# Other SBUF addresses for the same program: feed-forward buffers at multiples of 2048 bytes, attention buffers at multiples of 128

## The chip, the cores and the metric

The kernel runs on one core of a Trainium2 chip. A core has a matrix engine (TensorE, in the profile PE, with its weight loads listed apart as PEld), a vector engine (VectorE, DVE), a scalar engine (ScalarE, ACT), GpSimd (POOL), and a sync engine (SP) that here issues all the DMA transfers. The engines work on the on-chip memory SBUF, 128 partitions that are addressed alike: the address of a buffer is a byte offset that is the same in every partition. TensorE writes its results to a second memory, PSUM, in eight banks. The metric is the device time of one launch in microseconds (us); lower is better.

## What is computed

A linear attention over 8 batches, 8 heads, 576 positions and 64 channels, whose result feeds a gated feed-forward layer on 4608 tokens (512 to 1536 to 512). Everything is float32.

```python
def phi(x):
    proj = np.einsum('bhsd,df->bhsf', x, w_phi)
    proj = proj - np.max(np.abs(proj), axis=-1, keepdims=True)
    return np.concatenate([np.exp(proj), np.exp(-proj)], axis=-1)
q_p, k_p = (phi(q), phi(k))
kv = np.einsum('bhsf,bhsd->bhfd', k_p, v)
z = np.sum(k_p, axis=2)
num = np.einsum('bhsf,bhfd->bhsd', q_p, kv)
den = np.einsum('bhsf,bhf->bhs', q_p, z)[..., None] + 1e-06
attn = num / den
# x: attn as 4608 tokens of 512 channels
gate = 1.0 / (1.0 + np.exp(-(x @ w_gate)))
val = x @ w_val
out = gate * val @ w_out
```

## The kernel before

The work is cut in two kinds. Attention: 32 steps, one for a batch and a pair of heads (`attention(i)`). Its matmuls are float32: `pk` and `pq` (projections of k and q), `kvz` (kv and z), `tp` (transposes), `nm` and `dp` (numerator and denominator), `px` (spreading of maxima). Feed-forward: 9 chunks of 512 tokens by 12 blocks of 128 hidden channels (`unit(S_, C, j)`). Every operand is split into a high and a low part of type float32r, x into `xh` and `xl`, the weights into `wh` and `wl`, the hidden values into `hh` and `hl`, and three products stand for one: high by high, high by low, low by high. A matmul of the feed-forward has a stationary operand of 128 columns (512 bytes of a partition), which is loaded first, and a moving operand of 512 columns (2048 bytes). A unit has 12 matmuls for the gate (`g`), 12 for the value (`v`), which hold the weights still and move x (line 755), and then 12 for the output (`acc`, line 762), which hold `hh` or `hl` still and move the weights. That makes 9 x 12 x 36 = 3888 float32r matmuls of one size.

Blocks 0 to 3 are stage A: their weights `wh0` to `wl3` are made ready early, and their units fill TensorE between the steps of the attention. Blocks 4 to 11 are stage B (2592 of the 3888 matmuls); it comes when the attention is over. In the trace `gA`, `vA`, `hhA` belong to stage A and `gB`, `vB`, `hhB` to stage B. After a matmul of the gate come, on ACT and DVE, a tanh, an exp and some products (lines 797 to 824).

The order of all instructions is set when the program is built: the class `Plan` places each operation on its engine by ranks, given costs and due times, and emits them in that order. Costs and ranks don't depend on addresses.

SBUF is divided from two sides. From the left come `const` (with `ebias`), `moe` (x, t, u, hh, hl, y) and `wp1` (`wh0` to `wl3`), later replaced by four buffers `y2`. From the right come the buffers of the attention (`at1`, `at`). When the attention is done, `swap_right` gives these up and puts the weights of stage B (`wh4` to `wl11`) and their raw forms (`wraw`, `wtop`) in their place. A buffer starts at the end of its neighbour, rounded up to 32 bytes, so that one small buffer sets the remainder of all that follow. These are the addresses that come out:

| buffers | address before | remainder by 2048 / by 128 | address after | remainder by 2048 / by 128 |
|---|---|---|---|---|
| `xh`, `xl` (two of each, 8192 bytes each) | from 2208 | 160 / 32 | from 2048 | 0 / 0 |
| `t`, `u`, `hh`, `hl`, `y` of stage A (2048 each) | from 34976 | 160 / 32 | from 34816 | 0 / 0 |
| `wh0` ... `wl3` (6144 each), later `y2` | from 65696 | 160 / 32 | from 65536 | 0 / 0 |
| `wh4` ... `wl11` (6144 each) | 118752 to 217055 | 2016 / 96 | 116736 to 215039 | 0 / 0 |
| `wraw`, `wtop` of stage B | from 217056 | 2016 / 96 | from 215040 | 0 / 0 |
| `kin`, `qin`, `vin`, `wraw` and `mid` of stage A | from 121440 | several / 96 | from 118528 | several / 0 |
| `d`, `dk`, `ek`, `mb`, `kvt`, `eq`, `kv`, `ex`, `dr`, `rb`, `xp` | from 152864 | several / 32 | from 151296 | several / 0 |
| `mx`, `pm`, `pn`, `dn` (small) | from 152672 | several / 0, 32, 64 or 96 | from 149760 | several / 0 |
| `ident`, `ones`, `halves`, `wk`, `spread` | from 225888 | several / 96 | from 225536 | several / 0 |

The slices that matmuls of the feed-forward take of these buffers start at multiples of 512 bytes within them, so that a slice has the remainder of its buffer by 512, by 128 and by 64.

The functions that the diff touches:

Of the kernel before, what the change touches and what calls it, by code (L numbers as in the profile page):

```python
# [9 lines left out]
F32 = mybir.dt.float32  # L10
# [11 lines left out]
P = 128  # L22
# [8 lines left out]
HS = S // 2  # L31
Q = 32
# [122 lines left out]
def act_time(n):  # L155
    return 0.085 + n * 0.00085
# [3 lines left out]
def attention_moe(  # L160
# [10 lines left out]
    nc = tc.nc  # L171
    vec, act, pool = nc.vector, nc.scalar, nc.gpsimd
# [2 lines left out]

    const = ctx.enter_context(tc.tile_pool(name="const", bufs=1))
    dram = ctx.enter_context(tc.tile_pool(name="dram", bufs=1, space=DRAM))
    moe = ctx.enter_context(tc.tile_pool(name="moe", bufs=2))
    left, right = ExitStack(), ExitStack()
    wp1 = left.enter_context(tc.tile_pool(name="wp1", bufs=1))  # L180
    at1 = right.enter_context(tc.tile_pool(name="at1", bufs=1, side="right"))
    at = right.enter_context(tc.tile_pool(name="at", bufs=2, side="right"))
# [3 lines left out]
    homes = {"wp": wp1, "ws": at}  # L186
# [7 lines left out]
    def buf(tag, n):  # L194
        return Buf(rings.setdefault(tag, Slots(n)))
# [7 lines left out]
    ]  # L203
    dens = [dram.tile([2, S], F32, tag=f"den{i}", name=f"den{i}") for i in range(N)]

    ebias = const.tile([P, 1], F32, name="ebias")
    vec.memset(ebias, -896.0 * 2.0**23)
    ident = at1.tile([P, P], F32, name="ident")
    make_identity(nc, ident)
    ones = at1.tile([P, Q], F32, name="ones")  # L210
    vec.memset(ones, 1.0)
    halves = at1.tile([P, 2, Q], F32, name="halves")
    vec.memset(halves, 0.0)
# [2 lines left out]
    wk = at1.tile([P, F], F32, name="wk")  # L216
    nc.sync.dma_start(wk, w_phi)
    spread = at1.tile([P, 4, P], F32, name="spread")
    pool.memset(spread, 0.0)
    for a in range(4):  # L220
        qs = slice(a * Q, a * Q + Q)
# [5 lines left out]
    def head(hd):  # L227
        return slice(hd * D, hd * D + D)
# [102 lines left out]
    def attention(i):  # L331
        b, p = steps[i]
        n = f"{i}"
        T = {}
# [34 lines left out]
        mx, dk = buf("mx", 2), buf("dk", 1)  # L369
        eks = []  # L370

        def k_max():
            T["mx"] = [at.tile([P, 4], F32, tag=f"mx{g}", name=f"mx{n}_{g}") for g in range(3)]
            for g, ns in enumerate((4, 4, 1)):
                vec.tensor_reduce(
                    T["mx"][g][:, :ns], pks[g].t[:, :ns, :], axis=AX.X, op=ALU.max,
                    apply_absolute_value=True,
                )

        def k_sub():  # L380
            T["dk"], T["ek"] = [], []
            for g, ns in enumerate((4, 4, 1)):
# [6 lines left out]
                T["dk"].append(dkt)  # L389

        km = plan("DVE", 1.43, k_max, [ko], pks, [mx], rank=i)
        kb = plan("DVE", 1.43, k_sub, [km], [*pks, mx], [dk], rank=i)

# [66 lines left out]
        pm, mb = buf("pm", 2), buf("mb", 1)  # L460
        nj = 2 * S // Q

        def q_max():
            T["pm"] = at.tile([P, nj], F32, tag="pm", name="pm" + n)
            T["pn"] = at.tile([P, nj], F32, tag="pn", name="pn" + n)
            vec.tensor_reduce(
                T["pm"],
                T["d"].rearrange("p h s -> p (h s)").rearrange("p (j t) -> p j t", t=Q),
                axis=AX.X, op=ALU.max, apply_absolute_value=True, apply_transpose=True,
            )  # L470
# [30 lines left out]
        def q_sub():  # L501
            vec.tensor_tensor(T["d"], T["d"], T["mb"], op=ALU.subtract)

        q1 = plan("DVE", 1.38, q_max, qc, [d], [pm], rank=i)
        if perm:
            pp = Buf(banks, mine)
# [119 lines left out]
        if soon:  # L626

            def invert():
                dn = at.tile([P, 2 * HS // Q], F32, tag="ds", name="ds" + n)
                for hf, dp in enumerate(dps):  # L630
                    vec.tensor_reduce(
                        dn[:, hf * 9 : hf * 9 + 9], dp.t.rearrange("p (j t) -> p j t", t=Q),
                        axis=AX.X, op=ALU.max, apply_transpose=True,
                    )
                vec.tensor_scalar(dn, dn, 1e-6, None, op0=ALU.add)
                vec.reciprocal(dn, dn)
                T["rb"] = at.tile([P, S], F32, tag="rb", name="rb" + n, bufs=1)
                vec.transpose(T["rb"], dn.unsqueeze(2).broadcast_to([P, S // Q, Q]))

            r = [plan("DVE", 2.1, invert, [do], dps, [rb], rank=i - 1)]  # L640
        else:
            dr, dn = buf("dr", 1), buf("dn", 2)

            def den_copy():
                T["dr"] = at.tile([P, HS], F32, tag="dr", name="dr" + n, bufs=1)
                act.copy(T["dr"], dps[0].t)

            def den_in():
                T["dn"] = at.tile([P, 9], F32, tag="dn", name="dn" + n)
                nc.sync.dma_start(T["dn"], T["dr"].rearrange("(o r) c -> o r c", r=Q)[:, 0, :])  # L650

            def den_inv():
                vec.tensor_scalar(T["dn"], T["dn"], 1e-6, None, op0=ALU.add)
                vec.reciprocal(T["dn"], T["dn"])

            def den_out():
                nc.sync.dma_start(dens[i].rearrange("h (r c) -> (h r) c", c=9), T["dn"])

            def den_wide():
                T["rb"] = at.tile([P, S], F32, tag="rb", name="rb" + n, bufs=1)  # L660
                for hd in range(2):
                    nc.sync.dma_start(
                        T["rb"][head(hd), :], dens[i][hd].unsqueeze(0).broadcast_to([D, S])
                    )

            r = plan("ACT", act_time(HS), den_copy, [do], dps, [dr], rank=i - 0.2)
            r = plan("SP", 0.06, den_in, [r], [dr], [dn], rank=i - 2.5, mode=4)
            r = plan("DVE", 0.42, den_inv, [r], [dn], rank=i - 1)
            r = plan("SP", 0.06, den_out, [r], [dn], rank=i - 2.5, mode=4)
            r = [plan("SP", 0.12, den_wide, [r], [], [rb], rank=i - 2.5, mode=288, lag=2.5)]  # L670
# [172 lines left out]

    def swap_right():
        right.close()
        ctx.enter_context(reopen)
        for name in ("ws", "wp"):
            homes[name] = ctx.enter_context(
                tc.tile_pool(
                    name=name + "2", bufs=2 if name == "ws" else 1, side="right",  # L850
                    reuse_waits="tile",
                )
            )

    reopen = ExitStack()
    firsts = [o for n in range(3 * JA) for o in wdone[wtiles[n]]]
    swap = plan(None, 0.0, swap_right, [*every, *(s for c in stores.values() for s in c), *firsts])
    for n in range(3 * JA, 3 * NJ):
        weigh(n, 60 + n, swap)

    ydone, outs = {}, []
    for C in range(NCK):
# [5 lines left out]
        for t in range(CW // P):  # L868
            ab, yb = Buf(banks, apart), buf("y", 2)
            T = {}  # L870
# [30 lines left out]
    for C in range(NCK):  # L901
# [3 lines left out]
        for j in js:  # L905
# [3 lines left out]
            for t in range(CW // P):  # L909
# [15 lines left out]
                T = {}  # L925
# [15 lines left out]
                a = plan("DVE", vec_time(DM), add, [o, l], [accs[t], yb], rank=GATE)  # L941
                plan("SP", 0.06, store, [a], [yb], rank=90, mode=256)
    plan.run(trace)
    reopen.close()


# [53 lines left out]
```

## Time and profile before

| what | value |
|---|---|
| median of 3 runs | 1242.1 us (1240.03 to 1245.85) |
| the profiled execution | 1241.6 us, of which the span from first to last instruction is 1239.6 us |
| PE busy | 1220.3 us (98%), 8480 matmul instructions |
| DVE / ACT busy | 758.1 us (61%) / 518.1 us (42%) |
| DMA | 131.4 MB, mean 106 GB/s |
| granted TensorE clock, mean | 0.997 |

By the trace the attention, with stage A between its steps, lasts until 520 us, what is left of stage A until 616 us, and stage B from there to the end. Times in the views are microseconds from the start of the span. A matmul's duration in a row includes the time that its results need to run through the array (389 to 398 ns in the feed-forward); the next one starts long before. What a matmul costs is therefore read as the distance from one start to the next, called spacing below: where a row gathers twelve matmuls in sequence, it is a twelfth of its time.

### The profile page before, as it was taken

The numbers are of one execution on the slowest core, as the hardware profiler recorded it, in microseconds if no ns is written. First come the engines' busy times: TensorE is split into PE (matmuls) and PEld (weight loads), VectorE is DVE, ScalarE is ACT, GpSimd is POOL, SyncE is SP. The second block draws the span as 40 slices with busy tenths as digits, with TensorE's granted clock in tenths as the row PEclk, the third lists the DMA queues.
The fourth block names the chain that finished last, engine by engine and source line by source line (L and its number), as shares of the span: only waits on it lengthen the run. The fifth ranks groups of instructions, "written<-read, shape, count | busy, mean of one in ns | idle before, by whom it ended". The sixth has DMA issues, their size and how long they took to land.

```text
span 1239.6 us, 20852 instructions
## 1 busy us (share of the span) xinstructions
PE 1220.3 (98%) x8480; PEld 916.4 (74%) x8480; DVE 758.1 (61%) x1410; ACT 518.1 (42%) x1012; POOL 2.3 (0%) x11
## 2 busy tenths in 40 slices
PE   8999999999999999999999999999999999999998
PEld 6566766666666666688887888888888888888886
DVE  6989688889886889569986424333242434242333
ACT  6766566665575656544432212222222212221221
POOL 0000000000000000000000000000000000000000
PEclk9999999999999999999999999999999999999999
DMA  7776433443252533256662202011120202020100
GB/s 256 241 252 220 137 116 120 139 137 93 89 179 62 159 106 109 67 214 212 206 210 93 103 1 102 1 54 49 34 69 1 102 1 102 1 102 1 68 1 34
DMA packets 66891, 131.42 MB, mean 106 GB/s; under 512 B 16492, under 2 KB 22764, under 8 KB 64620
## 3 DMA queue, kind: packets, MB, share of 16 engines
q1 hardware_dynamic: 66796, 130.10, 32.0%
q8 instruction: 66, 1.08, 0.4%
q14 instruction: 29, 0.24, 0.1%
HBM read 92.04 MB, written 28.45 MB: 97 GB/s over the span
## 4 chain that ended last, share of the span: by engine, by line
PE 84%; DVE 10%; ACT 3%; issue 2%; DMA 1%; SPq 0%; DVEq 0%; ACTq 0%
PE acc L762 20%; PE vB L755 15%; PE gB L755 15%; PE gA L755 6%; PE vA L755 6%; PE kvz L534 5%; PE nm L592 5%; PE pq L434 3%; PE dp L616 2%; PE pk L360 2%; PE kvz L551 2%; DVE wtop L283 1%; DVE wraw L298 1%; ACT wtop L279 1%; PE tp L572 1%
## 5 line engine op out<-in xcount | busy, mean ns | idle before, releaser
L809 DVE SCALAR_TENSOR_TENSOR tB<-tB,vB 128x512 f32<-128x512 f32 x72 | 49.5, 687 | 208.0 <-PE vB L755 208.0
L820 ACT CAST hhB<-uB 128x512 fp32r<-128x512 f32 x72 | 44.7, 620 | 304.1 <-DVE uB L813 304.1
L762 PE MATMUL acc<-wh,hhB 128*128 128x512 f32 x288 | 114.5, 398 | 2.2 <-ACT hhB L820 2.2
L762 PE MATMUL acc<-wh,hlB 128*128 128x512 f32 x288 | 114.2, 397 | 0.7 <-DVE hlB L824 0.7
L762 PE MATMUL acc<-wl,hhB 128*128 128x512 f32 x288 | 114.5, 397 | 0.0
L755 PE MATMUL gB<-xlB,wh 128*128 128x512 f32 x288 | 113.8, 395 | 0.0
L755 PE MATMUL gB<-xhB,wl 128*128 128x512 f32 x288 | 113.7, 395 | 0.0
L755 PE MATMUL vB<-xhB,wl 128*128 128x512 f32 x288 | 113.6, 394 | 0.0
L755 PE MATMUL gB<-xhB,wh 128*128 128x512 f32 x288 | 113.6, 394 | 0.0
L755 PE MATMUL vB<-xhB,wh 128*128 128x512 f32 x288 | 113.5, 394 | 0.0
L755 PE MATMUL vB<-xlB,wh 128*128 128x512 f32 x288 | 113.5, 394 | 0.0
L797 ACT ACTIVATE tB<-gB 128x512 f32<-128x512 f32 x72 | 43.0, 598 | 130.5 <-PE gB L755 130.5
L805 DVE TENSOR_SCALAR tB<-tB 128x512 uint32<-128x512 uint32 x72 | 30.7, 426 | 104.6 <-ACT tB L797 104.6
L399 ACT ACTIVATE ek<-dk 128x512 f32<-128x512 f32 (+1 forms) x192 | 83.0, 519 | 9.2 <-DVE dk L384 9.2
L534 PE MATMUL kvz<-ek,vin 128*32 128x256 f32 x1280 | 75.5, 381 | 2.1 <-ACT d L446 2.1
L824 DVE TENSOR_TENSOR hlB<-uB,hhB 128x512 fp32r<-128x512 f32 x72 | 49.7, 691 | 41.2 <-ACT hhB L820 41.2
L762 PEld LDWEIGHTS acc<-wh,hhB 128*128 128x128 f32 x288 | 54.6, 190 | 15.4 <-ACT hhB L820 2.7
L762 PEld LDWEIGHTS acc<-wh,hlB 128*128 128x128 f32 x288 | 54.6, 189 | 14.7 <-DVE hlB L824 2.0
L755 PEld LDWEIGHTS gB<-xhB,wh 128*128 128x128 f32 x288 | 54.0, 188 | 13.2
L762 PEld LDWEIGHTS acc<-wl,hhB 128*128 128x128 f32 x288 | 54.5, 189 | 12.5
L755 PEld LDWEIGHTS vB<-xhB,wh 128*128 128x128 f32 x288 | 53.9, 187 | 13.3
L755 PEld LDWEIGHTS gB<-xlB,wh 128*128 128x128 f32 x288 | 54.0, 187 | 13.1
(114 smaller groups left out, 2459.2 us busy)
## 6 DMA issues: line engine op xcount, KB each, us to landing
wraw<-w_moe SPq DMA_DIRECT2D x36, 512.0 KB
kin<-k SPq DMA_DIRECT2D x32, 320.0 KB
vin<-v SPq DMA_DIRECT2D x32, 320.0 KB
qin<-q SPq DMA_DIRECT2D x32, 288.0 KB
wh<-wtop SPq DMA_DIRECT2D x36, 256.0 KB
ys<-y SPq DMA_DIRECT2D x36, 256.0 KB
xlB<-xs SPq DMA_DIRECT2D x9, 1024.0 KB
y<-ys SPq DMA_DIRECT2D x36, 256.0 KB
```

The source lines that it names most:

```text
L360: nc.tensor.matmul(pks[hd].t[:, t, :], kx[head(hd), t * P : t * P + P], wk[head(hd), :], start=True, stop=True,)
L399: act.activation(e[:, :, sg * F : sg * F + F], T["dk"][g], AF.Exp, scale=1.0 - 2.0 * sg,)
L434: nc.tensor.matmul(pqs[hd].t, wk[head(hd), :], T["qin"][head(hd), hf * HS : hf * HS + HS], start=True, stop=True,)
L534: nc.tensor.matmul(z[o : o + Q, : 2 * F], vx[:, 2 * t + hd, o % D : o % D + Q], (e0, e1)[hd][:, t, :] if t < 4 else e2[:, 0, :], start=t = ...
L592: nc.tensor.matmul(nm.t[o : o + Q, :], w[:, sg, o : o + Q], es[sg][:, o // D, cs], start=sg == 0, stop=sg == 1, tile_position=(0, o),)
L755: nc.tensor.matmul(o, a[:, ws], y[:, cs], start=i == 0, stop=i == 11)
L762: nc.tensor.matmul(acc, a[:, ts], w[:, ws], start=first and i == 0, stop=last and i == 2)
L797: act.activation(T["t"], gb.t, AF.Tanh, scale=0.5)
L805: vec.tensor_scalar(tu, tu, 0x7FFFFFFF, None, op0=ALU.bitwise_and)
L809: vec.scalar_tensor_tensor(t, t, 1.0, vb.t, op0=ALU.add, op1=ALU.mult)
L820: act.copy(T["h"][0], T["u"])
L824: vec.tensor_tensor(hl, T["u"], hh.bitcast(F32), op=ALU.subtract)
```

## The change

No operation is added or taken away but for padding: `ebias` becomes a slice of a 896-byte buffer and is allocated first; the scratch area for DMA descriptors at address 0 shrinks from 2048 to 1024 bytes; small buffers (`mx`, `pm`, `pn`, `dn`, `ds`, `ones`) become slices of 256-byte buffers and `dr` of one of 1280 bytes; two unused buffers (`edge`, 224 bytes, and `edge2`, 2016 bytes) stand at the right end. The sequence of instructions on each of the five engines is the same before and after, row for row. Five instructions, at the hand-over from the attention's buffers to those of stage B, wait on a partly different set of semaphores, since other old buffers lie under the new ones: three on DVE (on `wtop4_0`, `wraw4_0`, `wtop4_1`) and two transfers on SP (the loads of `wraw4_0` and of `xlA8`, chunk 8 of x).

```diff
+    ebias = const.tile([P, 224], F32, name="ebias")[:, :1]
+    vec.memset(ebias, -896.0 * 2.0**23)
     moe = ctx.enter_context(tc.tile_pool(name="moe", bufs=2))
...
-    ebias = const.tile([P, 1], F32, name="ebias")
-    vec.memset(ebias, -896.0 * 2.0**23)
     ident = at1.tile([P, P], F32, name="ident")
     make_identity(nc, ident)
-    ones = at1.tile([P, Q], F32, name="ones")
+    ones = at1.tile([P, 2, Q], F32, name="ones")[:, 0, :]
...
     spread = at1.tile([P, 4, P], F32, name="spread")
+    at1.tile([P, 56], F32, name="edge")
...
-            T["mx"] = [at.tile([P, 4], F32, tag=f"mx{g}", name=f"mx{n}_{g}") for g in range(3)]
+            T["mx"] = [
+                at.tile([P, 64], F32, tag=f"mx{g}", name=f"mx{n}_{g}")[:, :4] for g in range(3)
+            ]
...
-            T["pm"] = at.tile([P, nj], F32, tag="pm", name="pm" + n)
-            T["pn"] = at.tile([P, nj], F32, tag="pn", name="pn" + n)
+            T["pm"] = at.tile([P, 64], F32, tag="pm", name="pm" + n)[:, :nj]
+            T["pn"] = at.tile([P, 64], F32, tag="pn", name="pn" + n)[:, :nj]
...
-                dn = at.tile([P, 2 * HS // Q], F32, tag="ds", name="ds" + n)
+                dn = at.tile([P, 64], F32, tag="ds", name="ds" + n)[:, : 2 * HS // Q]
...
-                T["dr"] = at.tile([P, HS], F32, tag="dr", name="dr" + n, bufs=1)
+                T["dr"] = at.tile([P, 320], F32, tag="dr", name="dr" + n, bufs=1)[:, :HS]
...
-                T["dn"] = at.tile([P, 9], F32, tag="dn", name="dn" + n)
+                T["dn"] = at.tile([P, 64], F32, tag="dn", name="dn" + n)[:, :9]
...
     def swap_right():
         right.close()
-        ctx.enter_context(reopen)
+        edge = reopen.enter_context(tc.tile_pool(name="edge", bufs=1, side="right"))
+        edge.tile([P, 504], F32, name="edge2")
         for name in ("ws", "wp"):
-            homes[name] = ctx.enter_context(
+            homes[name] = reopen.enter_context(
...
-    reopen = ExitStack()
+    reopen = ctx.enter_context(ExitStack())
...
-    nc = bacc.Bacc("TRN2", target_bir_lowering=False, num_devices=1, dynamic_dma_scratch_size=2048)
+    nc = bacc.Bacc("TRN2", target_bir_lowering=False, num_devices=1, dynamic_dma_scratch_size=1024)
```

More of the change, by code (lines that the diff above doesn't have):

```diff
@@ L943, in attention_moe @@
     plan.run(trace)
-    reopen.close()
 def kernel(**inputs):
```

## The prediction

> **What bounds the kernel now.** I read the page first, then the busy times by stage, the chain of work, and the timeline at the places where stages meet.
>
> ```profile
> span 1239.6 us, 20852 instructions
> PE 1220.3 (98%) x8480; PEld 916.4 (74%) x8480; DVE 758.1 (61%) x1410; ACT 518.1 (42%) x1012; POOL 2.3 (0%) x11
> PE 84%; DVE 10%; ACT 3%; issue 2%; DMA 1%; SPq 0%; DVEq 0%; ACTq 0%
> ```
>
> TensorE is busy 98% of the span and is 84% of the chain that ends last. By stage (columns: length, then busy time and instructions of PE, PEld, DVE, ACT, POOL, then granted clock, DMA share, GB/s):
>
> ```profile
> 20.00:520.00 500.00, 492.35 (x5247) 329.32 (x5239) 414.78 (x823) 316.42 (x654) 0.00 (x0) 1.00 0.45 142
> 520.00:600.00 80.00, 79.93 (x355) 65.85 (x352) 63.50 (x118) 34.49 (x61) 0.00 (x0) 1.00 0.55 189
> 700.00:1200.00 500.00, 500.00 (x2150) 402.91 (x2149) 182.87 (x298) 116.25 (x205) 0.00 (x0) 1.00 0.14 47
> ```
>
> In the attention PE is busy 492 of 500 us and DVE 415, from then on PE without a gap at full granted clock. In stage B, DVE (183 of 500) and ACT (116) have room to spare. So the time is the number of matmuls times their spacing, and a change of addresses acts through the spacing or not at all. The spacing is not one number:
>
> ```profile
> 533.94 2.72 PE gA L755 x12
> 539.38 5.45 PE acc L762 x24
> 673.07 2.80 PE vB L755 x12
> 675.87 2.80 PE gB L755 x12
> 681.47 2.79 PE acc L762 x12
> ...
> 692.62 2.80 PE gB L755 x12
> ```
>
> These are pieces of the chain (start, length, twelve or twenty-four matmuls). At the end of stage A a matmul costs 2.72 / 12 = 226.7 ns (5.45 / 24 = 227.1 in the output), in stage B 2.80 / 12 = 233.3, with the same shape, type and clock. From the row of 700 to 1200 us: 500.00 / 2149 = 232.7 ns, the mean of stage B. What differs? First, the other engines in two such pieces:
>
> ```profile
> 533.94:536.66 2.72, 2.72 (x13) 2.25 (x13) 1.38 (x2) 0.00 (x0) 0.00 (x0) 1.00 0.99 401
> 673.07:675.87 2.80, 2.80 (x13) 2.25 (x13) 0.00 (x0) 0.00 (x0) 0.00 (x0) 1.00 0.00 0
> ```
>
> The quick piece has the DMA engines at 99% and DVE at half; in the slow one nothing runs but PE. The surroundings are not the cause. Second, the place where it turns (start, duration):
>
> ```profile
> 615.00 0.39 PE L762 MATMUL acc<-wl,hhA 128*128 128x512 f32 x1
> ...
> 615.90 0.39 PE L762 MATMUL acc<-wh,hlA 128*128 128x512 f32 x1
> 616.13 0.40 PE L755 MATMUL gB<-xhB,wh 128*128 128x512 f32 x1
> ...
> 617.30 0.39 PE L755 MATMUL gB<-xhB,wl 128*128 128x512 f32 x1
> ```
>
> Five spacings up to 616.13 make 1.13 us (226), the five after it 1.17 (234). It turns at the very first matmul whose weights lie in the buffers of stage B. What sets these apart in the table of addresses is the remainder by 128: 32 for x and the weights in stage A, 32 for x but 96 for the weights in stage B. The stationary operand of the next matmul is loaded while the present one reads its moving operand:
>
> ```profile
> 1227.85 0.39 PE L755 MATMUL vB<-xhB,wl 128*128 128x512 f32 x1
> 1227.85 0.19 PEld L755 LDWEIGHTS vB<-xhB,wh 128*128 128x128 f32 x1
> ```
>
> Both start at 1227.85. Two reads of SBUF run side by side, and how they lie to each other seems to cost 6 ns a matmul. Third, the end of the kernel, where the granted clock has fallen to half:
>
> ```profile
> 1232.49:1234.62 2.13, 2.13 (x6) 1.65 (x5) 1.30 (x2) 0.00 (x0) 0.00 (x0) 0.50 0.15 58
> 1232.49 0.63 PE L762 MATMUL acc<-wh,hhB 128*128 128x512 f32 x1
> ...
> 1234.20 0.63 PE L762 MATMUL acc<-wl,hhB 128*128 128x512 f32 x1
> ```
>
> Four spacings make 1.71 us, 427 ns each, of which half is 213.5. That is the spacing at full clock if nothing were in the way, 512 columns at 2.4 a nanosecond. So 13.2 ns in stage A and 19.2 in stage B are lost to something that vanishes when the array reads half as fast. That fits reads that get in each other's way.
>
> **The change part by part.** *The weights of stage B* come from remainder 96 to 0, x and h from 32 to 0: both operands then have equal remainders, as in stage A now. I take A's measured spacing: 232.7 - 226.7 = 6.0 ns, by 2592 matmuls, 15.6 us, all on the path, since PE has no gap there.
>
> *Stage A*: remainders equal before (32 and 32) and after (0 and 0). I take no change. Bounds: no row shows two operands at 0, so either way by one step of 6.0 over 1296 matmuls, 7.8 us, and down to 213.5 (13.2 x 1296 = 17.1).
>
> *Matmuls of the attention*, 8480 - 3888 = 4592 instructions:
>
> ```profile
> 517.46 0.67 PE L592 MATMUL nm<-d,kv 128*32 128x288 f32 x8
> 517.95 0.67 PE L592 MATMUL nm<-eq,kv 128*32 128x288 f32 x8
> 518.43 0.67 PE L592 MATMUL nm<-d,kv 128*32 128x288 f32 x8
> 518.92 0.67 PE L616 MATMUL dp<-eq,kv 128*32 128x288 f32 x8
> ```
>
> Eight take 1.46 / 3 = 0.487 us, four 243 ns. Four run at once in quarters of the array. At two passes over 288 columns 576 / 2.4 = 240 would be the least, so at most 3 ns in 243 can be won: 4592 / 4 x 3 = 3.4 us. I take 0, since slower reads seem to leave nothing to win; the opposite bound is the same 3.4.
>
> *DVE and ACT* read and write at new addresses too. In the attention DVE idles 85 of 500 us; that idle time hides a few per cent of change either way. If it were gone, each per cent of DVE's 415 us would cost 4 us. In stage B it would take DVE at more than twice its time. 0 taken.
>
> *Transfers*: all sizes and their order stay. What PE waits for a transfer is once, at the start:
>
> ```profile
> PE pk L360 <- DMA kin<-k: 4.3, 1, 4.3
> ```
>
> So between 0 and 4.3 us could be won there, and a transfer a tenth slower would cost 0.4. 0 taken. The smaller descriptor scratch holds nothing here: the page's queue table names only hardware and instruction queues.
>
> *The five changed waits* stand where the first weights of stage B are made. Behind the waiting loads on SP stand the next weight loads; who waits for those is DVE, then PE:
>
> ```profile
> L304 DVE SCALAR_TENSOR_TENSOR wl<-wraw x24: 691/693/696, 544.5 to 669.2; 128x512 fp32r<-128x512 uint32 x24
> 698.23 2.79 PE acc L762 x12
> ```
>
> The last low part of the weights is done at 669.9 and first used at 698.2 (its block comes last): 28 us of cover. Until then PE gains (698 - 616) x 6.0 / 232.7 = 2.1 us on them. Cover stays, cost 0; without it, each microsecond late is one at the end.
>
> *Padding, the earlier memset of `ebias`* (one instruction at the start, while the first load is awaited): 0.
>
> Sum, against the profiled execution's 1241.6 us (0.5 below the median of the runs): 1241.6 - 15.6 = 1226.0.
>
> **The rivals.** *The start in itself counts.* Stage A's 226.7 and B's 233.3 differ by 6.67 ns, 16 columns of four bytes, 64 bytes. If reads go in pieces of 64 bytes, a row of 2048 bytes that starts at remainder 32 or 96 touches 33 pieces, and one at 0 touches 32. Then A's spacing drops by 6.7 as well, to 220.0, and B's by 12.7: 12.7 x 2592 + 6.7 x 1296 = 41.6 us, 1200.0. For it: both spacings are multiples of 6.67 (34 and 35). Against it: no aligned matmul in the trace; the 64 bytes may as well be the length of a round of banks, in which only the two operands' difference matters.
>
> *All is lost to the start*: 213.5 everywhere, 19.2 x 2592 + 13.2 x 1296 = 66.9 us, 1174.7. Against it: one piece of 64 bytes is worth half of 13.2. The Trainium skill (TensorE: Matmul & The Clock Gate, Back-to-back issue gap) gives an isolated warm spacing of N / 2.4 + 2.5 ns, so 215.8 here; by it this rival would come to an estimated 1183.
>
> *No change*: it isn't the remainder but the region. The weights of stage A lie below 115 KB, those of B between 118 and 217 KB, before and after. Then 1241.6. For it: in the trace region and remainder change together, so nothing separates them. Against it: the piece at 675.87 reads block 10 of the first chunk (weights from 192 KB on) and the one at 692.62 block 4 of the second (from 118 KB on), and both take 2.80; a matter of region should show steps within B. The Trainium skill speaks for no change, too: SBUF — State Buffer (Specifications) has lines of 16 bytes, of which 32 and 96 are multiples, and the Trainium skill's TensorE: Matmul & The Clock Gate (Step-by-step: what each phase is for) says that loading the next weights doesn't take read bandwidth from the running matmul. The trace's 2.72 against 2.80 with nothing else running is not explained by either.
>
> *Slower*: if both reads starting on a boundary always hit the same bank first, equal remainders at 0 would cost a further step of 6.0 instead of saving one, in A as in B: 6.0 x 3888 = 23.3 us, 1264.9. It decides once B's spacing passes 232.7 + 6.2 / 2592 us = 235.1. Against it: A has equal remainders now and is the quicker stage.
>
> **How the numbers follow.** Equal remainders as in A (1226.0): 0.42, the only one with a measured spacing. The start itself (1200.0): 0.20. The full floor (1174.7): 0.08. No change (1241.6): 0.15. Slower (1264.9): 0.08. The remaining 0.07 are mixtures, 0.05 of them gains and 0.02 within the bound. A measurement of this kernel can tell about 0.5%, 6.2 us, from no change. Faster 0.42 + 0.20 + 0.08 + 0.05 = 0.75, no change 0.17, slower 0.08. The range leaves out the floor and the slower case (0.16) and goes from the start's 1200.0 less the 3.4 of the attention's matmuls, 1196, to the no-change case with the median's 0.5 and the same 3.4 as a loss, rounded down to 1244. The likeliest case's own range is 1218 to 1234 (A's step of 7.8 either way).
>
> **What would show it.** In the changed profile's chain, twelve matmuls of `gB` and `vB` at 2.72 us, and 500 us of stage B holding some 2205 of them instead of 2149: right. 2.64 in both stages: the start itself counts. 2.80 in B: region. Above 2.82: the slower case. The attention should still end near 520 us and stage B begin near 616; if these move, stage A's spacing or DVE has changed. I am wrong if the difference between the operands isn't what the step at 616.13 came from, or if an absolute start matters, which nothing before can show.

## The result, and the profile after

The changed kernel takes 1229.8 us (median of 4 runs, 1227.1 to 1232.4), the kernel before beside it 1242.2 (4 runs, 1240.0 to 1245.9). The ratio is 0.9897, 95% interval 0.9865 to 0.9929: 12.4 us less. The profiled execution took 1229.7 us. From its page, the span, the busy times and the chain's shares:

```profile
span 1227.8 us, 20852 instructions
PE 1204.3 (98%) x8480; PEld 916.1 (75%) x8480; DVE 757.1 (62%) x1410; ACT 517.2 (42%) x1012; POOL 2.3 (0%) x11
PE 82%; DVE 10%; DMA 3%; ACT 3%; issue 2%; SPq 0%; DVEq 0%; ACTq 0%
```

PE is busy 16 us less with as many instructions; DVE and ACT are unchanged to about a microsecond. So the new addresses did next to nothing for those two, and what PE gained lies in its own instructions. The same stretches as before, by engine (length, then PE, PEld, DVE, ACT, POOL, clock, DMA share, GB/s):

```profile
20.00:520.00 500.00, 490.51 (x5227) 328.83 (x5223) 411.72 (x820) 314.35 (x651) 0.00 (x0) 1.00 0.45 141
520.00:600.00 80.00, 79.09 (x362) 64.30 (x351) 62.93 (x115) 33.93 (x62) 0.00 (x0) 1.00 0.53 184
700.00:1200.00 500.00, 500.00 (x2208) 414.01 (x2207) 187.02 (x304) 119.08 (x211) 0.00 (x0) 1.00 0.13 47
```

The last row holds 2207 weight loads where 2149 stood: 500.00 / 2207 = 226.6 ns, against 232.7. The prediction asked for "some 2205". In the chain, twelve matmuls of stage B now cost what twelve of stage A cost:

```profile
534.87 2.72 PE gA L758 x12
540.31 5.45 PE acc L765 x24
...
675.86 2.72 PE vB L758 x12
678.58 2.72 PE gB L758 x12
684.02 2.72 PE acc L765 x12
```

Stage A stayed at 2.72 and stage B came down from 2.80 to it. The step at the hand-over is gone; the timeline there:

```profile
617.24 0.39 PE L765 MATMUL acc<-wh,hhA 128*128 128x512 f32 x1
...
618.38 0.39 PE L765 MATMUL acc<-wh,hlA 128*128 128x512 f32 x1
618.60 0.39 PE L758 MATMUL gB<-xhB,wh 128*128 128x512 f32 x1
...
619.28 0.39 PE L758 MATMUL gB<-xhB,wh 128*128 128x512 f32 x1
```

Five spacings make 1.14 us up to 618.38, and four after it 0.90: 228 and 225 ns, equal to what two decimals tell. The spacing came out as predicted; the gain of the profiled span, 11.8 us, falls 3.8 short of the 15.6. Where these went is seen when the two traces are cut at the same matmuls (start times of matmuls, us):

| stretch | before | after | change | by the prediction |
|---|---|---|---|---|
| up to the last matmul of the attention | 519.7 | 520.6 | +0.9 | 0 |
| from there to the first matmul of stage B | 96.5 | 98.0 | +1.5 | 0 |
| from there to the first use of `hl` of block 8 (230 matmuls, 182 of them stage B's) | 54.4 | 54.7 | +0.3 | -1.1 |
| from there to the last matmul (2409) | 564.9 | 550.4 | -14.5 | -14.5 |
| from there to the end of the span | 4.1 | 4.1 | 0.0 | 0 |

From block 8 of the first chunk on, everything came out as predicted, to 0.1 us. Ahead of it something other than PE's spacing sets the time. The chain of the kernel before, just ahead of the cut at block 8:

```profile
669.15 0.69 DVE wl L304
669.85 0.61 DVE hlB L824
670.50 2.56 PE acc L762 x10
```

The same place in the chain of the changed kernel:

```profile
671.91 0.69 DVE wl L305
672.60 0.61 DVE hlB L827
673.26 2.60 PE acc L765 x10
```

Both come from DVE, which makes the last low part of the weights and only then the `hlB` that the output needs. A quicker PE gets there sooner and waits longer, as the table of PE's waits between 515 and 700 us says (total, times, longest). The one row of the kernel before:

```profile
PE acc L762 <- DVE hlB L824: 0.7, 1, 0.7
```

The rows of the changed kernel:

```profile
PE acc L765 <- DVE hlB L827: 1.1, 1, 1.1
PE gA L758 <- ACT y L883: 0.9, 1, 0.9
PE acc L765 <- ACT hhB L823: 0.6, 1, 0.6
PE acc L765 <- DVE tA L812: 0.5, 1, 0.5
```

The second and the fourth row stand in stage A, whose matmuls didn't get quicker. Their origin is a transfer. The chain of the changed kernel near 575 us:

```profile
573.04 7.79 DMA xlB<-xs
580.86 0.63 ACT xhB L733
581.51 1.07 DVE xlB L740 x2
```

The timeline of a later kernel with the same stage A (stage B's weights 256 bytes further, below), issue and use of the same transfer:

```profile
576.02 0.58 SPq L728 DMA_DIRECT2D xlB<-xs  x1
582.95 1.07 DVE xlB L740 x2
```

From issue to DVE's use it is 8.47 us in the one and 6.93 in the other (6.9 in the kernel before, 572.12 to 579.00). Of the other profiled kernels below with this stage A and this issue, four show 6.9, and the ones with stage B's weights 64 and 128 bytes off show 7.39 and 7.95. With 6.9 the stretch of the table lasts 96.4 to 96.5 us, as before; with 7.39, 7.95 and 8.47 it lasts 97.0, 97.5 and 98.0, so that it grows by what the transfer takes longer. So 1.5 us of the missing 3.8 are a transfer that came late in this execution; five kernels with the same addresses in stage A do without the delay, and two have part of it.

### The profile page after: what moved, and what is told of

Read it like the earlier page. It is cut to its first block, busy times and chain, and to the rows that moved or that the text cites. A ratio compares the mean times of both kernels' runs of the same rounds, so it can differ in the third digit from the quotient of the medians.

```text
span 1227.8 us, 20852 instructions
## 1 busy us (share of the span) xinstructions
PE 1204.3 (98%) x8480; PEld 916.1 (75%) x8480; DVE 757.1 (62%) x1410; ACT 517.2 (42%) x1012; POOL 2.3 (0%) x11
## 4 chain that ended last, share of the span: by engine, by line
PE 82%; DVE 10%; DMA 3%; ACT 3%; issue 2%; SPq 0%; DVEq 0%; ACTq 0%
PE acc L765 20%; PE vB L758 15%; PE gB L758 15%; PE gA L758 6%; PE vA L758 6%; PE kvz L537 5%; PE nm L595 5%; PE pq L437 3%; PE pk L361 2%; PE dp L619 2%; PE kvz L554 1%; DVE wtop L284 1%; ACT wtop L280 1%; DVE wraw L299 1%; DMA rb<-den 1%
## 5 line engine op out<-in xcount | busy, mean ns | idle before, releaser
L765 PEld LDWEIGHTS acc<-wl,hhB 128*128 128x128 f32 x288 | 54.3, 189 | 11.4
L537 PEld LDWEIGHTS kvz<-ek,vin 128*32 128x32 f32 x1280 | 39.4, 110 | 31.3 <-issue 4.3
L758 PEld LDWEIGHTS vB<-xlB,wh 128*128 128x128 f32 x288 | 54.1, 188 | 11.3
```

The costliest lines, as they stand in the source:

```text
L537: nc.tensor.matmul(z[o : o + Q, : 2 * F], vx[:, 2 * t + hd, o % D : o % D + Q], (e0, e1)[hd][:, t, :] if t < 4 else e2[:, 0, :], start=t = ...
L758: nc.tensor.matmul(o, a[:, ws], y[:, cs], start=i == 0, stop=i == 11)
L765: nc.tensor.matmul(acc, a[:, ts], w[:, ws], start=first and i == 0, stop=last and i == 2)
```

## The experiments

The theory was the prediction's: the remainders of the two operands that TensorE reads side by side have to agree. The rivals: the start on a multiple of 64 or 2048 counts in itself; the region of SBUF counts; or something else in the change (the attention's small buffers, the five waits). Spacings in this part are means of start-to-start times in the trace, with waits (280 ns and more) left out.

### One padding alone

The kernel before, with nothing but 1856 bytes at the right end, so that the weights of stage B come to remainder 160 by 2048, where x has stood all the time:

```diff
+EDGE = 464
...
+        edge = reopen.enter_context(tc.tile_pool(name="edge", bufs=1, side="right"))
+        edge.tile([P, EDGE], F32, name="edge2")
```

> The kernel before with one padding buffer of 1856 bytes at the right end after the hand-over, so that the weights of stage B lie at remainder 160 by 2048 (32 by 128), as x and h do already; nothing else moves, the attention stays at remainders 32 and 96. Theory D (only the difference of the two operands' remainders counts): spacing in stage B 226.7 ns, time about 1229 us, the same as the changed kernel. Theory S (the start itself must be a multiple of 64 or 128 too, and the attention's addresses help): B stays above 228 ns and the time between 1234 and 1242 us.

Measured 1228.2 us beside 1241.5, ratio 0.9907 (0.9889 to 0.9925), with the spacing of stage B at 226.7 ns:

```profile
700.00:1200.00 500.00, 500.00 (x2208) 414.06 (x2207) 186.49 (x303) 118.03 (x208) 0.00 (x0) 1.00 0.13 47
```

This is the stretch of 700 to 1200 us, with the 2207 loads of the changed kernel. The whole gain is there without one multiple of 2048 and without a change to the attention's buffers. This refutes the start in itself and the other parts of the change as its source.

### The changed kernel with stage B's weights 64 bytes off

```diff
-        edge.tile([P, 504], F32, name="edge2")
+        edge.tile([P, 504 - 16], F32, name="edge2")
```

> The changed kernel, with only the padding at the right end 64 bytes shorter, so that the weights of stage B lie at remainder 64 by 128 while x, h and all of stage A stay at 0. Theory D by 128: spacing of the gate and value in B back to 233.3 ns, of the output to about 231.7, time about 1242 us. Theory S with pieces of 64 bytes, or D by 64: nothing changes, 226.7 ns and about 1230 us. Theory R (any shift of the right side matters through buffers that overlap, not through remainders): no forecast of the spacing, but waits instead.

Measured 1241.0 us, ratio 1.0005 (0.9992 to 1.0017). The stretch of 700 to 1200 us:

```profile
700.00:1200.00 500.00, 500.00 (x2150) 402.99 (x2149) 183.61 (x299) 115.93 (x205) 0.00 (x0) 1.00 0.13 47
```

2149 loads, the figure of the kernel before (its gate and value at 233.3 ns). All of the gain hangs on these 64 bytes; 64 is a multiple of 16, of 32 and of 64, so no alignment of single operands to any of these is what counts. The run says something about the rest of the change, too: this kernel has all its other new addresses, and in stage B the same difference as the kernel before (weights less x is 64 modulo 256 in both). So the other addresses together are worth between 1 us won and 2 us lost, by the interval of the ratio.

### Eight differences in one kernel, twice

Small paddings between the blocks of stage B give each block another difference between its weights and x. In the first kernel x is at remainder 0, in the second x, `hh`, `hl` and the weights of stage A are at 32.

```diff
+PAD = {5: 8, 6: 8, 7: 8, 8: 8, 9: 16, 10: 16, 11: 16}
...
+                if PAD.get(j):
+                    homes["wp"].tile([P, PAD[j]], F32, tag=f"pad{j}", name=f"pad{j}")
```

> The changed kernel with small paddings between the weights of stage B: blocks 4 to 11 at differences of 0, 32, 64, 96, 128, 192, 256 and 320 bytes to x and h, which stay at multiples of 2048. One run gives a table of spacing by difference. Theory D by 128: 226.7 ns at 0, 128 and 256, 233.3 at 64, 192 and 320, something of their own at 32 and 96. D by 256 or 512: 226.7 only at 0 and 256, or only at 0. Theory S: 226.7 wherever the remainder by 64 is 0, more at 32 and 96. Time between 1232 and 1240 us, as the blocks mix.

> As the sweep before, with x, h and the weights of stage A shifted by 32 bytes (remainder 32), so that the same absolute places of the weights make differences of -32, 0, 32, 64, 96, 160, 224 and 288. Theory D by 128: the table is the same function of the difference: 226.7 at 0 (block 5), 233.3 at 64 (block 7) and the values of 32 and 96 from the sweep before at the others; 160 and 288 as 32, 224 as 96. Theory S: no block reaches 226.7 as a moving operand at remainder 32 pays one piece more, or those at 0 of their own keep what they had.

One run each, 1240.5 and 1243.9 us. Spacing of `g` and `v` by the difference (weights less x, bytes), without the first and the last of each twelve:

| difference | -32 | 0 | 32 | 64 | 96 | 128 | 160 | 192 | 224 | 256 | 288 | 320 |
|---|---|---|---|---|---|---|---|---|---|---|---|---|
| x at 0 | | 227.7 | 233.2 | 233.3 | 234.2 | 232.4 | | 231.2 | | 227.2 | | 233.3 |
| x at 32 | 233.3 | 228.7 | 233.2 | 233.3 | 234.1 | | 233.8 | | 233.3 | | 232.4 | |

The commonest values at 0 and 256 are 226 and 227. Where the block ahead has another difference, the first few matmuls of a twelve, up to seven, take between 223 and 241 ns before the row settles at these; that lifts the means. In the chain of the first kernel, by the order of its blocks, these are differences of 96, 256, 0 and 64:

```profile
725.16 2.81 PE vB L761 x12
747.42 2.72 PE vB L761 x12
764.04 2.72 PE vB L761 x12
777.87 2.80 PE gB L761 x12
```

Quick and slow blocks lie side by side in the same region, which refutes that rival. And stage A with both operands at 32 ran at 226.9 ns, as at 0 (227.0). So it is the difference that counts and not the place, and of the multiples of 128 tried 0 and 256 are good, not 128, by which the front part's table gave the remainders.

### 256 bytes off, and 128

The same line as above, with `504 - 64` and with `504 - 32`.

> The changed kernel with the weights of stage B 256 bytes further up (remainder 256 by 2048), all else as it is. If the difference counts by 256, as the sweeps suggest: 226.7 ns all through stage B and the changed kernel's time, about 1229 us. If it counts by 512 or 2048 and the 227.2 of the sweep's block 10 was a leftover: 231 to 234 ns, about 1240 us.

> The same with 128 bytes: equal remainders by 128, unequal by 256. Difference by 256: spacing 232 to 233.3 ns, about 1240 us, no gain over the kernel before. Difference by 128: 226.7 and about 1229 us.

At 256: 1229.6 us, ratio 0.9885 (0.9855 to 0.9915). At 128: 1243.5, ratio 1.0012 (0.9997 to 1.0027). The chain at 256:

```profile
728.69 2.72 PE gB L758 x12
731.41 2.72 PE vB L758 x12
734.13 2.72 PE acc L765 x12
```

The chain at 128:

```profile
729.83 2.80 PE gB L758 x12
732.63 2.80 PE vB L758 x12
735.43 2.80 PE acc L765 x12
```

So 256 bytes off is as good as 0, and 128 is as bad as 64: as far as these kernels go, the difference counts modulo 256.

### Finer differences

Blocks at differences below 32 bytes, on both sides of 0, to see whether any place is better than 0 (`OFF` counts words of 4 bytes, modulo 256 bytes).

```diff
+OFF = {4: 1, 5: 2, 6: 4, 7: 6, 8: 56, 9: 60, 10: 62, 11: 63}
...
+                    weights[j] += (t[:, o % 8 : o % 8 + 3 * DM],)
```

> The changed kernel with the weights of blocks 4 to 11 at differences of 4, 8, 16, 24, -32, -16, -8 and -4 bytes to x by 256. If the quick place is one exact address: about 233 ns at all of them. If it is a band as wide as a line of 16 or 32 bytes: 226.7 at 4 and 8 (and 16 and 24), or somewhere less than 226.7, which would point to a better address than 0.

One run, 1241.3 us. Means of `g` and `v`: +4 bytes 232.2 ns, +8 231, +16 233.3, +24 230.0, -4 229, -8 233, -16 229, -32 233. There is no simple course, and no mean is below 226.7. A difference of 16 bytes, a whole line by the Trainium skill (SBUF — State Buffer, Specifications), costs the full 6.6 ns; that page's lines do not explain it.

The means at -4 and -16 hide two levels. Two pieces of the chain, both of block 11 (-4 bytes):

```profile
753.64 2.79 PE gB L768 x12
759.20 2.73 PE vB L768 x12
```

By the start times, in all nine chunks the `v` rows of this block run at 227 ns from their first matmul to the eleventh, and the `g` rows settle at 233. At -16 both settle at 227, after three matmuls in `g` and six in `v`. So the quick spacing occurs at small differences other than 0, too, and at -4 bytes quick and slow rows stand at the same difference. What decides between them there is not shown.

### Which pair of operands

In the changed kernel the low weights `wl` of stage B are put 128 bytes off, the high ones stay at 0. Then one of three products multiplies unequal operands.

```diff
+                    if swap:
+                        homes["wp"].tile([P, 32], F32, tag=f"p{x}{j}", name=f"p{x}{j}")
```

> The kernel after, with the low-order weights of stage B (wl4 to wl11) 128 bytes further by 256 than the high-order ones (wh4 to wh11); x, and with it xh and xl, stays at 0, wh at 0. Of the three products of a block, in order wh by xh, wl by xh and wh by xl, only one multiplies weights and a moving operand at different remainders by 256. If what counts is the pair that one matmul multiplies, one matmul in three is long: two at 226.7 ns and one at 233.3 ns, 686.7 ns for three, a mean of 228.9 ns over stage B, and about 1229.8 + 2592 x 2.2 / 1000 = 1235.5 us in all; the long one is the one whose weights are wl. If what counts is the weight load of the following matmul that runs beside this one's moving reads, the long one is the matmul ahead of it, and the total is the same 1235.5 us. If one unequal pair upsets the row of them, all three are at 233.3 ns and the total is near 1243 us. If the remainder by 256 of the high-order weights alone set the rate, nothing moves: 226.7 ns and 1229.8 us.

One run, 1238.2 us. In `g` and `v`, where the weights are the loaded operand, two of three spacings are long: `xh` by `wh` 226.7 ns, `xl` by `wh` (while `wl` is being loaded) 232.5, `xh` by `wl` 234.2. In the output, where the weights are the moving operand and `hh`, `hl` (at 0) are loaded, one is long: 226.8, then `wl` 234.1, then 225.9. In the chain:

```profile
728.24 2.77 PE gB L761 x12
731.02 2.77 PE vB L761 x12
733.79 2.75 PE acc L768 x12
```

Four times the sums of three make 2.774 and 2.747. So neither of the two simple forms is right alone: in this kernel a matmul is long if its moving operand differs from the weights that are loaded beside it, and also if it differs from its own weights, which are already in the array; both at once don't add up (the output's `wl`). That the second comes from the matmul's own weights is not shown apart from an after-effect of the load just ahead of it; in the output the matmul behind the long one is not slowed (225.9). The expected total of 1235.5 was for one long matmul in three; two in `g` and `v` give 1728 x 4.4 + 864 x 2.2 = 9.5 us, 1239.3.

### Less to load

If the reads of the loaded weights take time from the moving operand, a narrower load should cost less. In blocks 6 to 11 of the changed kernel the second and third product hold 64 or 32 columns instead of 128, and the rest of these low-order terms is left out of the result.

```diff
+                n = WIDE.get(j, P) if i % 3 and i < 11 else P
...
+                    o[:n], a[:, ws][:, :n], y[:, cs], start=i == 0, stop=i == 11,
```

> The changed kernel, with two of three products of blocks 6 to 11 in stage B holding still only the first 64 (blocks 6, 7, 10, 11) or 32 (blocks 8, 9) of their 128 columns, so that the low-order terms of the rest are left out; the moving operand stays at 512 columns. If the 13.2 ns over 213.5 are weight loads that get in the way of the moving operand's reads, a matmul beside whose reads a half or a quarter weight load runs has about 220 or 217 ns, and 226.7 where the load is full. If they are a fixed cost of a matmul of this type, or of a weight load as such: 226.7 with every width.

One run, 1235.0 us. A load took 188, 134 and 108 ns for 128, 64 and 32 columns, but the spacing did not fall as expected. In `g` and `v` it is 227.2 ns with full loads (blocks 4 and 5). A matmul that holds all 128 columns while a load of 64 runs beside it took 226.8 (220 was expected), beside a load of 32 it took 230 (217 expected). A matmul that holds 64 beside a load of 64 took 231.7, one that holds 32 beside a load of 32 took 232.5. The prediction's picture, a loss in proportion to the reads of the load, is not borne out. What the 13.2 ns are that stay above 213.5 at equal remainders is open.

### Stage A put off instead

The changed kernel with 64 bytes ahead of stage A's weights, so that A is unequal and B equal.

```diff
+    gap = left.enter_context(tc.tile_pool(name="gap", bufs=1))
+    gap.tile([P, 16], F32, name="gap")
```

> The kernel after, with the weights of stage A (wh0 to wl3) at 64 by 256 and all else as in the kernel after, x at 0 and the weights of stage B at 0. If the difference of the two addresses counts wherever they lie, stage A's matmuls from the end of the attention on go from 226.7 to about 233.3 ns: 467 of them by 6.6 ns, 3.1 us; the matmuls that run between the attention's steps (230.2 ns) may rise by up to as much, at most 829 x 6.6 = 5.5 us more. Total 1233 to 1238 us, the time before coming back by a quarter to two thirds although stage B is untouched at 226.7 ns. If it is the region in which stage B's weights lie that counts, stage A stays at 226.7 ns and the total at 1229.8 us.

Measured 1230.9 us, ratio 0.9907 (0.9873 to 0.9941). The spacing did what the theory says, 2.80 us for twelve in stage A's gate and value:

```profile
552.33 2.80 PE gA L760 x12
...
569.13 2.80 PE gA L760 x12
...
574.73 11.00 PE acc L767 x48
```

233.3 ns (226.9 in the kernel before), also between the attention's steps (230.3 before, 233.2 now). The output went only to 229, although stage B's output took 231.7 with its weights 64 bytes off; so the difference alone doesn't fix the size of the loss. B stayed at 226.7. But the total rose by only 1.1 us over the changed kernel's, less than the intervals can tell apart, where 3 to 8 were expected. From the attention's end to stage B it took 98.0 us, 1.5 more than the 96.5 of most kernels: the slower matmuls add 2.1 us, and waits of PE at stage A's matmuls fell from 0.7 us (the kernel before) to 0.1. PE had some slack in stage A, and the slower matmuls used it up first. The attention itself ended at 521.1 us, no later than in kernels with a quick stage A.

### The cover taken away

Who sets the time between 546 and 673 us? In all twelve kernels above, quick and slow ones, the 230 matmuls ahead of block 8's `hl` took 54.3 to 54.7 us. One of DVE's passes over the raw weights of stage B is cut to 16 of 512 columns, in the changed kernel and in the kernel before; most signs of these weights are left out of the result.

```diff
+            n = 16 if swap else DM
             vec.scalar_tensor_tensor(
-                top, words("raw", 1), 0x80000000, top,
+                top[:, :n], words("raw", 1)[:, :n], 0x80000000, top[:, :n],
```

> The kernel after, with one of DVE's passes over the raw weights of stage B (the one that puts the signs back, 24 times 0.70 us) cut to 16 of 512 columns; the other signs are left out of the result. Its point: from the first matmul of stage B to the first use of hl of block 8 (230 matmuls, 182 of them stage B's) the kernels so far took 54.3 to 54.7 us, whether their matmuls took 226.7 or 233.3 ns. If it is DVE's work on the weights that sets this stretch, it falls, with 16.8 us less for DVE between 544 and 672 us, to TensorE's own 230 x 226.7 ns = 52.1 us and a few tenths of waiting; the 96.5 us from the attention's end to stage B's first matmul fall to about 95.4; what follows block 8 stays at 550.4. Total some 3 us below the kernel after. If the stretch is bound otherwise (by transfers, by the start of the rows of matmuls), it stays at 54.5.

> The same edit in the kernel before (most signs of stage B's weights left out). If DVE sets the stretch, it falls to 182 matmuls at 232.7 ns and 48 at 226.7, 53.2 us, and a few tenths: 1.1 us above the same stretch of the changed kernel with the same edit, where the two kernels without the edit differ by nothing. What follows block 8 stays at 564.9. All of stage B then differs between the two addresses by the predicted 15.6 us instead of 14.2. If the stretch is bound otherwise, the two stay equal at 54.5 and stage B differs by 14.4.

One run each, 1224.4 and 1238.7 us. The stretch took 52.13 us with the new addresses and 53.29 with the old ones; the rest 550.2 and 564.6. Stage B as a whole now differs by 15.5 us (602.3 against 617.9 from its first to its last matmul), where it differed by 14.2 (605.1 against 619.3). The whole times differ by 14.2, since the attention ended 1.7 us later in the run with the new addresses; these are single runs. The 96.5 us ahead of stage B fell to 95.7 in both. No wait of PE is left between 520 and 700 us in either, and the chain runs through PE where DVE and ACT stood. The new addresses:

```profile
605.51 10.88 PE acc L766 x48
616.39 2.72 PE gB L759 x12
619.11 2.72 PE vB L759 x12
```

The old addresses:

```profile
603.81 10.88 PE acc L763 x48
614.68 2.80 PE gB L756 x12
617.49 2.80 PE vB L756 x12
```

This shows the missing term: 1.1 to 1.4 us of the gain were hidden behind DVE (the stretch differs by 1.2 now, where it differed by 0.3 the other way).

## Why the prediction was right, and where it wasn't

**What bounds the kernel.** Right in the main: spacing times count. The claim that all of stage B's 15.6 us lie on the path "since PE has no gap there" failed for the first 55 us. The chain of before ran through DVE and ACT there; the rows of 669.15 to 670.50 above are from it. A busy share of 98% hid that.

**Stage B's spacing.** 226.7 ns taken from stage A's rows, 226.7 measured; 14.5 us from block 8 on, as worked out. The step that chose the measured spacing of the equal case over a computed one was the good one. What was inferred from the table, remainders by 128, was the wrong reading: 128 bytes off costs everything, 256 nothing. That the change went to a difference of 0, which is good by either reading, was luck: by the prediction a move to 128 would have promised the same 15.6 us, and it gains nothing. The picture behind it, reads that get in each other's way, is not shown: the narrower loads speak against a loss in proportion to the load, and why the difference counts stays open.

**Stage A.** 0 taken; 226.9 ns before, 227 after, and 230.3 in the attention both times.

**The cover of the weights.** This is the term that was mis-sized. The prediction looked at the last low weights (28 us of cover) and called the cost 0. But the same DVE queue makes `hlB`, with no cover at all: the row of `hlB` waits grew from 0.7 to 1.1 us, waits at block 6 came up, and the 182 matmuls in that stretch gained nothing instead of 1.1 us. With less work on DVE they gained it.

**Transfers.** "0 taken", with a bound at the start of the kernel alone. A transfer of x (`xlB`) near 575 us came 1.5 us late in the profiled execution and moved everything behind it, because DVE and PE both wait for it. It varies between executions: five kernels with the same addresses in stage A don't show it, two show a part.

**The attention, DVE and ACT.** 0 taken, +0.9 us measured. Between executions the attention ends at 519.9 to 523.6 us with the new addresses of its buffers (eleven profiled executions, mean 521.4), and at 518.8 to 520.0 with the old ones (three, mean 519.5). That could be a small loss, and the one padding alone is 1.5 us below the changed kernel by their medians, but the intervals of the two ratios overlap. The kernel with stage B's weights 64 bytes off, against the kernel before, bounds it at about 2 us. Whether there is a loss is left open. The prediction's own bound for the attention's matmuls, 3.4 us, took all 4592 as running four at once, which it had read off `nm` and `dp` alone.

**The rivals.** The start in itself: refuted (all the gain with x and weights at 160, and 226.9 ns in stage A with both at 32). Region: refuted (quick and slow blocks next to each other). The slower case did not come. The floor of 213.5 at full clock was not reached by any kernel. The estimate by the Trainium skill's formula (TensorE: Matmul & The Clock Gate, Back-to-back issue gap), 215.8 ns, was missed by 10.9 in the best of them. The Trainium skill's rule that a weight load doesn't take read bandwidth from the running matmul (TensorE: Matmul & The Clock Gate, Step-by-step: what each phase is for) does not account for the product of `xl` and `wh`: it took 226.9 ns in the changed kernel and 232.5 where only `wl`, loaded beside it, lay 128 bytes off. Only at the end, where the granted clock is 0.50, does the spacing come out at 2 x 213.5, with the old addresses and with the new. The timeline of the changed kernel:

```profile
1220.68 0.63 PE L765 MATMUL acc<-wh,hhB 128*128 128x512 f32 x1
...
1222.39 0.63 PE L765 MATMUL acc<-wl,hhB 128*128 128x512 f32 x1
```

Four spacings in 1.71 us, 427 ns, as before.

## What to carry to other kernels

Where rows of 128x512 float32r matmuls run without gaps, compare the addresses of the stationary and the moving operand: a difference of 0 or 256 bytes gave 226.7 ns here, the means of all others tried were 229 to 234, and one padding buffer was enough to get it; alignment in itself gave nothing. To size such a gain, cut the trace at the same instructions in both kernels and ask of each stretch what its chain runs through: a stretch whose chain runs through another engine gives nothing back, however busy PE looks. And before a microsecond is blamed on a change, look whether a kernel with the same addresses shows it too.

## What the runs showed of the hardware that was not expected

- The cost of unequal operands went by the difference modulo 256 bytes; in `g` and `v` it is about 6 ns in 226.7 at 32, 64 or 128, less in the mean at some small differences (-4 and -16, where quick rows of 227 ns occur), and no mean is below 226.7. A row of matmuls keeps a trace of the block ahead: it can take up to seven matmuls to settle.
- With the low weights 128 bytes off, an unequal stationary operand slowed two matmuls, the one beside which it is loaded (232.5 ns) and the one that uses it (234.2); an unequal moving operand slowed one (234.1).
- Narrower weight loads (134 and 108 ns instead of 188) made the matmuls that hold them slower, not quicker, where another narrow load runs beside them: 231.7 and 232.5 ns against 227.2. No run here explains this.
